# An inverse DFT with its operand, its copies and its last stage laid out anew

## The chip, the cores and the metric

The kernel runs on one core of one Trainium2 chip. The metric is the device time of one execution in microseconds. The core has a matrix engine (TensorE, in the profile PE, with its weight loads as PEld), a vector engine (VectorE, DVE), an activation engine (ScalarE, ACT), GpSimd (POOL) and SyncE (SP), which here only issues DMAs. Each engine works through its own queue in order; engines wait for one another by semaphores.

## The reference, cut to what matters

`u` is 2048 positions by 512 channels. A layer norm gives `xn`; a state-space convolution and a one-token expert run on it, and their product is added to `u`.

```python
x = A_u
xn = _layernorm(x, axis=-1)
# s: long convolution of each channel with a kernel K of 2048 taps
dt = jnp.exp(log_dt)[:, None]
P = jnp.exp((dt * A)[:, :, None] * l[None, None, :])
K = jnp.einsum("dn,dnl,dn->dl", Cc, P, dt * Bc).real
Yf = rfft(pad(xn.T)) * rfft(pad(K))
s = irfft(Yf)[..., :L].T + xn * Dskip
# g: silu of xn, where the one token with the highest router score got an FFN added
g = _silu(_B_ref(xn, w_r, w_gate, w_up, w_down))
return x + s * g
```

## The kernel before

All Fourier transforms are matrix products. The 512 channels are worked on in two halves, h = 0 and 1, of 4 x 64 channels (in the code, q counts the four groups of 128 channels, and h is a half of each group). The stages, in the order of the data:

- **norm, router, ffn** give the normalised rows, the chosen row and the gate operand G, which goes through DRAM (`scr_g`).
- **useq, useq2** transform the input in two steps and leave its spectrum in DRAM (`scr_u`); `load_u(h)` brings a half back into `UU[h]`: for each of 32 residues k2, real and imaginary parts on 128 partitions, and a second copy (t = 1) with the two parts exchanged. For h = 0 both copies come by DMA; for h = 1 one comes by DMA and eight on-chip copies make the other.
- **tab, exp, g, q, qc, mm** (together "kgen") build K for each half on ScalarE, VectorE and TensorE; **kx** turns it into the operand `KX[h]`.
- **spec** (`spec(h, ...)`): for each pair of residues kp (16 of them) ten 128x256 matmuls of the table FD with KX give the spectrum of K in a PSUM bank, an evacuation copies it to `KF`, and VectorE multiplies it with UU (stage uum). For h = 0 the product is written over UU, 1024 elements in one instruction; for h = 1 it goes to `Y1` in four instructions of 256 elements, where the columns of one channel lie 4 elements apart.
- **inv** (`inv_a(h)`): the first step of the inverse. For each of 64 channels m two matmuls (t = 0, 1), whose weights are the 128 columns of that channel and whose moving operand is a 128-column table, write every fourth word of a bank; after eight channels four copies of 64 partitions by 512 elements bring the pair of banks to `C`.
- **fin** (`fin_h(h)`): the last step. For each position l1 sixteen matmuls on four column tiles, of 128 rows and 64 columns; the table FB has zeros in half of its rows, so that two groups q share one operand. Then ScalarE copies the result (`TB`), VectorE multiplies by silu(G) and adds the input row (`XR`), and for h = 1 four DMAs per block store 32 partitions each.

`_Graph` records each operation with its buffers and works out the waits from the overlaps of addresses; buffers are placed by hand at offsets from `RA`, `RX`, `RM`, `RQ0`, `RQ1`, `RT`, `RG`, so that two buffers of different stages often share a place, and a write waits for the last read of what lay there. Helpers issue everything, so that lines of the profile are those of helpers: `mm` is L647, `tt` L598, `act` L593, `evac` L626 on ScalarE or L627 on VectorE, `dma` L664. The order of each engine's queue is a table of operation numbers, `ORDER`, made beforehand by a planner from estimated costs. In it fin0 stands within spec1 and inv1, and `g.schedule` only checks it.

Of the kernel before, what the change touches and what calls it, by code (L numbers as in the profile page):

```python
# [16 lines left out]
KB = 1024  # L17
# [323 lines left out]
def tables():  # L341
# [28 lines left out]
    FZ = np.zeros((2, 2, 32, 64, 2, 32))  # L370
    for q in range(2):
        FZ[:, q, :, :, q] = FB.transpose(2, 0, 1, 3)
    FB = FZ.reshape(128, 64, 2, 32)
# [6 lines left out]
        9 8 10 3-4 19 14 13 20 16 15 216 18 212 17 214 148 144 149-150 146 102 97 100 151 147 101 99 143 142 96 145 95 98 155 157 154 156 152-153 222  # L380
        224 218 220 226 228 230 232 236 238 234 240 250 252 242 254 316 256 258 321 260 708 264 262 326 331 709 336 268 341 270 266 346 710 351 711
        713-714 278 712 851 808 804 806-807 803 805 1006 1005 1004 1014 1016 1015 1025 1028 1026 1003 1052 1017 1027 1038 1051 1041 1040 1039""",
    scalar="""
        2 6 5 7 12 11 21 53-54 22 29 55 26 25 30 24 27 57-59 46 450 440 425 34 31 33 444 38 446 435 48 426 452 454 443 424 37 442 439 430 136 449 88
# [4 lines left out]
        592 579 597 578 575 340 338 500 598-599 570 628 577 590 587 574 588 600 345 343 514 576 520 581 348 518 350 595 586 522 596 582 524 584 572  # L389
        528 530 532 534 672 716 719 722 725 639 728 731 643 641 734 737 645 743 740 749 746 755 686 688 761 752 690 758 692 854 698 696 764-765 771  # L390
        700 769-770 776 775 704 777 781-782 786 811-812 789 792 790 879 810 873 794 891 801 885 809 897 802 915 909 797 927 921 939 933 951 823 945
        830 957 959-960 837 963 969 968 972 975 977 980 984 983 989 988 992 848 993 1000 1011 1022 1035 1048 1053-1054""",
    vector="""
        0-1 211 105 103 106 113 104 111 66 71 28 112 107 109 23 117 56 110 62-63 108 118 68 114 65 116 115 64 61 119 36 67 60 70 69 120 32 72 121 73
        122 74 123 75 84 124 76 125 77 126 78-79 127 131 80 128 81 129 82 130 132 83 133-134 85 137-139 86 135 140-141 87 91 90 92-93 89 94 161 164
        159 167 170 173 362 360 364 179 359 367 283 368 184-185 361 186 369 363 373 457 374 188 379 456 376 459 380 190 458 191-193 460 462 385 195
        461 388 464 463 197 466 198-200 465 375 467-468 202 469-472 386 473 205 474 476 475 210 477-478 274-275 479-482 309 484 488 485 506 486-487
        490 489 505 483 503 491-492 244 247 494 493 507 498 245 508 330 496 509-510 246 335 249 203 511-512 603 606 604 607 605 609 516 608 610-611
        671 613 612 615 614 616-617 619 618 673 621 630 620 622-623 625 624 626-627 526 629 631 633 632 272 635 276 634 277 674 636-637 646-647 649
        648 650-654 656 655 658 657 535 660 659 662 661 664 663 676 666 665 675 668 667 670 669 678 677 679-680 682 681 684 683 729 741 726 732 717  # L400
        747 735 744 762 720 738 723 759 753 750 756 857 694 853 766-767 855 859 772 774 706 858 702 852 707 779 784 780 787 785 867 791 871 861 856
        862-863 796 814 880-881 870 883 865 882 868 864 818 875 869 816 876 795 894 892 874 877 815 903 895 817 905 887 906 886 889 888 799 898 800
        900-901 899 893 912 904 913 910 930 911 907 925 929 924 922 916 941 940 942 918 917 923 934 931 919 928 943 937 953 955 954 952 936 824 935
        946 948 947 949 825 831-832 958 964 962 965 967 970 974 973 979 978 982 985 987 990 994 838 995 839 849-850 1001-1002 1012-1013 1023-1024
        1049-1050 1036-1037""",
    gpsimd="""
        447 390 389 536-537 42 39 41 40 43-44 594 279""",
    tensor="""
        45 47 158 160 163 166 162 169 165 172 168 171 175 178 174 181 49 177 282 51 180 183 286 187 290 280 189 294 284 194 298 196 288 302 201 292
        204 306 296 206-209 310 300 213 215 217 304 219 221 223 308 225 227 229 231 314 312 233 235 319 317 237 324 239 322 241 243 327 497 329 495  # L410
        332 501 334 499 337 339 515 344 251 253 255 519 342 513 349 347 257 259 517 261 263 521 525 523 527 529 531 533 265 267 269 271 715 718 721
        724 638 727 730 642 640 733 736 644 742 739 748 745 754 685 687 760 751 689 757 691 697 695 693 763 768 699 773 705 701 703 778 783 860 866
        788 813 793 878 872 798 890 884 902 896 914 908 926 920 938 932 950 819-822 944 826-829 956 961 833-836 966 840 842 841 843-845 971 976 981
        986 991 846-847 996-999 1007-1010 1018-1019 1031 1020-1021 1032 1029-1030 1033-1034 1044-1045 1042-1043 1046-1047""",
# [7 lines left out]
def build(nc, A_u, A_A_re, A_A_im, A_B_re, A_B_im, A_C_re, A_C_im, A_log_dt, A_Dskip,  # L422
# [52 lines left out]
    with g.ctx:  # L475
# [80 lines left out]
        G0 = g.buf("G0", RQ1 + 16 * KB, [4, 2, 16, 64], BF16)  # L556
        FB = g.buf("FB", RQ1 + 32 * KB, [64, 2, 32], BF16)
# [8 lines left out]
        VM = g.buf("VM", RT, [4, 512], BF16)  # L566
        WR4 = g.buf("WR4", RT + 9 * KB, [128], BF16)
        WRC = g.buf("WRC", RT + 9 * KB + 256, [4], BF16)
        KF = [g.buf(f"KF{i}", RT + 9 * KB + 1024 * i if i < 3 else RQ0 + 37 * KB + 1024 * (i - 3) if i < 8 else RM + 1024 * i, [4, 128], BF16) for i in range(16)]
# [608 lines left out]
        spec(0, range(16), FD, 0)  # L1178

        g.stage = "inv0"  # L1180
        inv_a(0)
        g.stage = "ldz"
        load(FB(FB.a.reshape(-1)), t_fb.ap(), 128 * 8192)
        g.stage = "ldg"
# [109 lines left out]
```

## Time and profile before

| | us |
|---|---|
| median of 3 runs | 220.4 (218.86 to 221.02) |
| profiled execution | 220.46 |
| its span, first to last instruction | 218.6 |
| TensorE busy | 166.0 (76%) |
| VectorE busy | 189.4 (87%) |
| ScalarE busy | 161.3 (74%) |

Times in the views run from the start of the span. A row of a timeline has start, length, engine, line, operation, output and operands, the shape, and how many instructions are merged. `128*20 128x42` at a matmul are the weights' rows and columns and the moving operand's rows and columns. Matmuls overlap, so the slot of one in a stream is what counts: the length of the stream less one duration, by the number less one. The granted clock is the share of TensorE's full clock.

The end of the kernel by the chain of waits is TensorE from 123 us on, then the copies and products of the last step, then the stores.

### The profile page before, as it was taken

The page shows a single profiled execution, that of the slowest core. Times are in us where ns is not written, and L with a number is a line of the kernel's source. Part 1 is how long each engine was busy: PE and PEld are TensorE (multiplying, and loading weights), DVE is VectorE, ACT ScalarE, POOL GpSimd, SP SyncE. Part 2 cuts the span into 40 slices and gives each one's busy share as a digit, 9 for nine tenths or more (in the row PEclk, how much of TensorE's full clock was granted, in tenths as well). Part 3 has the DMA queues.
Part 4 walks back from the last instruction along what each step waited for, and adds up shares of the span by engine and source line. Part 5 has one row for each costly group of instructions (what it writes and reads, how often), then busy time and mean ns, then how long its engine had stood idle before and what let it go on. Part 6 is the DMA issues. An engine that isn't in the chain of part 4 may idle for free.

```text
span 218.6 us, 6958 instructions
## 1 busy us (share of the span) xinstructions
PE 166.0 (76%) x2995; PEld 134.7 (62%) x2995; DVE 189.4 (87%) x408; ACT 161.3 (74%) x318; POOL 13.8 (6%) x17
## 2 busy tenths in 40 slices
PE   0150787799868768879957499989999997999440
PEld 0140676573654346657746488889889886988330
DVE  3999988998999999999999999476779999767970
ACT  2899999999999999999722144464689977556630
POOL 2021430000000000000000620000000000000000
PEclk9995555555965559999988799997999999999755
DMA  6990579700455896969999972059980000000076
GB/s 216 396 374 0 138 142 200 294 3 0 151 178 175 232 352 177 308 179 264 310 286 213 363 294 108 3 126 390 208 240 3 3 0 4 3 0 3 3 199 187
DMA packets 21142, 36.76 MB, mean 168 GB/s; under 512 B 1944, under 2 KB 16888, under 8 KB 20088
## 3 DMA queue, kind: packets, MB, share of 16 engines
q1 hardware_dynamic: 20120, 35.60, 54.2%
q10 hardware_dynamic: 960, 0.72, 1.0%
q8 instruction: 23, 0.38, 0.7%
q14 instruction: 7, 0.06, 0.1%
q0 software_dynamic: 32, 0.00, 0.0%
HBM read 25.83 MB, written 8.39 MB: 157 GB/s over the span
## 4 chain that ended last, share of the span: by engine, by line
PE 41%; DVE 35%; ACT 13%; issue 5%; DMA 2%; SPq 0%; DVEq 0%
PE PB L647 41%; DVE TT L598 8%; DVE QQ L598 8%; DVE Y L598 4%; DVE GG L598 3%; ACT E L593 2%; DMA X<-in_A_u_dram 2%; DVE ST L760 2%; ACT AU L626 2%; ACT TB L593 2%; ACT SL L593 2%; DVE LST L616 1%; ACT XT L626 1%; DVE QQ L1024 1%; ACT QQ L593 1%
## 5 line engine op out<-in xcount | busy, mean ns | idle before, releaser
L647 PE MATMUL PB<-KX,FD 128*128 128x256 bf16 x320 | 38.7, 281 | 0.0
L647 PEld LDWEIGHTS PB<-KX,FD 128*128 128x128 bf16 x320 | 31.6, 101 | 5.8 <-ACT KX L626 0.4
L647 PE MATMUL PB<-QQ,GG 128*20 128x42 bf16 x1024 | 25.0, 263 | 9.7 <-DVE QQ L598 5.2
L647 PEld LDWEIGHTS PB<-QQ,GG 128*20 128x20 bf16 x1024 | 21.4, 124 | 13.5 <-issue 6.8
L627 DVE CAST C<-PB 64x512 bf16<-64x512 f32 x30 | 20.7, 689 | 9.5 <-PE PB L647 8.2
L626 ACT ACTIVATE C<-PB 64x512 bf16<-64x512 f32 x34 | 20.1, 592 | 11.9 <-PE PB L647 10.7
L626 ACT ACTIVATE KF<-PB 128x512 bf16<-128x512 f32 x29 | 17.3, 598 | 13.7 <-PE PB L647 12.9
L598 DVE TENSOR_TENSOR TT<-GG,MB 128x2048 bf16<-128x2048 bf16 (+3 forms) x32 | 24.3, 787 | 0.3
L593 ACT ACTIVATE QQ<-TH 128x256 bf16<-128x256 f32 x64 | 22.5, 427 | 0.0
L593 ACT ACTIVATE E<-AR 128x256 bf16<-128x256 f32 x64 | 22.3, 426 | 0.0
L598 DVE TENSOR_TENSOR QQ<-QQ,E 128x1024 bf16<-128x1024 bf16 (+2 forms) x16 | 19.6, 1252 | 0.0
L647 PE MATMUL PB<-CB,XZN 32*128 32x64 bf16 x256 | 15.8, 327 | 4.4 <-ACT AU L626 3.5
L647 PEld LDWEIGHTS PB<-CB,XZN 32*128 32x128 bf16 x256 | 12.8, 203 | 7.0 <-ACT AU L626 5.0
L647 PE MATMUL PB<-CB,UU 128*128 128x128 bf16 x128 | 17.0, 338 | 0.0
L626 ACT ACTIVATE KE<-PB 128x336 bf16<-128x336 f32 x13 | 6.0, 464 | 13.7 <-PE PB L647 13.7
L647 PE MATMUL PB<-AU,F2U 64*128 64x256 bf16 x128 | 12.6, 342 | 4.4 <-ACT UST L626 3.6
L647 PEld LDWEIGHTS PB<-CB,UU 128*128 128x128 bf16 x128 | 15.7, 185 | 0.4 <-issue 0.2
L598 DVE TENSOR_TENSOR GG<-TT 128x1024 bf16<-128x1024 bf16 (+3 forms) x38 | 15.1, 434 | 0.4
L647 PE MATMUL PB<-CB,Y 128*128 128x128 bf16 x128 | 14.6, 313 | 1.1 <-DVE Y L598 1.1
L626 ACT ACTIVATE AU<-PB 128x1024 bf16<-128x1024 f32 x14 | 14.2, 1041 | 0.5 <-PE PB L647 0.5
L647 PEld LDWEIGHTS PB<-CB,Y 128*128 128x128 bf16 x128 | 13.5, 137 | 1.6 <-DVE Y L598 1.2
L598 DVE TENSOR_TENSOR Y<-UU,KF 128x256 bf16<-128x256 bf16 x64 | 14.0, 283 | 0.4 <-ACT KF L626 0.3
(133 smaller groups left out, 287.5 us busy)
## 6 DMA issues: line engine op xcount, KB each, us to landing
FD<-c_fd SPq DMA_DIRECT2D x4, 1280.0 KB, 7.6
scr_u<-UST SPq DMA_DIRECT2D x8, 512.0 KB, 5.2
UU<-scr_u SPq DMA_DIRECT2D x2, 2048.0 KB, 15.4
XZN<-XN SPq DMA_DIRECT2D x16, 128.0 KB, 4.2
scr_g<-XN SPq DMA_DIRECT2D x4, 512.0 KB, 7.2
UU<-scr_u SPq DMA_DIRECT2D x2, 1024.0 KB, 11.3
XR<-in_A_u_dram SPq DMA_DIRECT2D x4, 512.0 KB, 14.6
G<-scr_g SPq DMA_DIRECT2D x1, 2048.0 KB
```

Source lines behind the costliest of these rows:

```text
L593: g.op(AC, lambda e: e.activation(out=out.ap, in_=in_.ap, func=func, **kw), w=[out], r=r, cost=cost(AC, out, 0.71), table=table, tokr=tokr ...
L598: g.op(eng, lambda e: e.tensor_tensor(out=out.ap, in0=a.ap, in1=b.ap, op=op), w=[out], r=[a, b], cost=cost(eng, out, rate))
L616: g.op(eng, lambda e: e.scalar_tensor_tensor(out=out.ap, in0=a.ap, scalar=x, in1=b.ap, op0=op0, op1=op1), w=[out], r=r, cost=cost(eng, out ...
L626: g.op(AC, lambda e: e.activation(out=out.ap, in_=in_.ap, func=ACT.Copy), w=[out], r=[in_], cost=cost(AC, out, 0.71) + 80, alt=(DV, lambda ...
L627: alt=(DV, lambda e: e.tensor_copy(out=out.ap, in_=in_.ap), cost(DV, out, 1.05) + 95))
L647: ins = e.matmul(o_.ap, lhsT=l_.ap, rhs=r_.ap, start=st, stop=sp, **kw)
L760: g.op(DV, lambda e, b=b: e.bn_stats(ST6(ST6.a[b]).ap, X0(X0.a[b]).ap), w=[ST6(ST6.a[b])], r=[X0(X0.a[b])], cost=620)
L1024: lambda e: e.tensor_scalar(out=out.ap, in0=in_.ap, scalar1=-1.0, scalar2=None, op0=ALU.mult), cost(DV, out, 0.3))
```

## The change

- The product with the spectrum is written, for both halves, to a new buffer `Y[h]` in the order [t, channel, q, k2]: the 128 columns of one channel are adjacent. Each of the 16 steps takes two instructions of 512 elements; the elements of a step lie 128 elements (256 bytes) apart in the output.
- The inverse reads `Y[h][t, m]`; its result is copied as 128 partitions by 1024 elements, with the last copy of h = 1 in two halves.
- The last step runs once, behind both halves: FB without zeros and repeated on four groups of 32 partitions, sixteen 32-row, 32-column tiles, with a moving operand of 2 x 64 columns; six blocks of 2 or 4 positions; one store of 128 partitions per block. The last product reads PSUM directly.
- Buffers have new places: Y0 at RM (where kgen's tables E, TH, MB lay), Y1 over UU0 and GG, C in the second halves of UU0 and UU1's places, UU1 at RQ1 (kgen's Q1) with its load in two parts, G0 in two parts and two loads, FB at RX + 8 KB, XR at RM (Y0's place), KF8 to 15 at RT (kgen's scratch TT).
- `ORDER` is new for all engines.

```diff
-    FZ = np.zeros((2, 2, 32, 64, 2, 32))
-    for q in range(2):
-        FZ[:, q, :, :, q] = FB.transpose(2, 0, 1, 3)
-    FB = FZ.reshape(128, 64, 2, 32)
+    FB = np.tile(FB, (4, 1, 1, 1))
...
-        C = apart("C", RM, RM2, [2, 64, 64])
-        Y1 = g.buf("Y1", RQ0, [2, 16, 4, 32, 4], BF16)
-        UU = [g.buf("UU0", RQ0, [2, 4, 32, 64], BF16), apart("UU1", RM2, RQ1, [4, 32, 64])]
+        C = apart("C", RQ0 + 16 * KB, RQ1, [2, 64, 64])
+        Y = [g.buf("Y0", RM, [2, 64, 4, 32], BF16), apart("Y1", RQ0, RG, [64, 4, 32])]
+        UU = [g.buf("UU0", RQ0, [2, 4, 32, 64], BF16), g.buf("UU1", RQ1, [2, 4, 32, 64], BF16)]
...
-                if h == 0:
-                    uv = uu(uu.a[:, :, 2 * kp:2 * kp + 2].reshape(2, 4, 128))
-                    tt(DV, uv, uv, kf(bc(kf.a[None], (2, 4, 128))), ALU.mult)
-                else:
-                    for kk in range(2):
-                        for t in range(2):
-                            k2 = 2 * kp + kk
-                            tt(DV, Y1(Y1.a[t][:, :, k2].transpose(1, 0, 2)), uu(uu.a[t, :, k2].reshape(4, 16, 4)), kf(kf.a[:, 64 * kk:64 * kk + 64].reshape(4, 16, 4)), ALU.mult)
+                for t in range(2):
+                    tt(DV, Y[h](Y[h].a[t, :, :, 2 * kp:2 * kp + 2].transpose(1, 2, 0)), uu(uu.a[t, :, 2 * kp:2 * kp + 2]), kf(kf.a.reshape(4, 2, 64)), ALU.mult, 1.05)
...
-                        lst.append((pr(pr.a.reshape(2, 128, 4)[i // 4, :, i % 4]), uu(uu.a[t, :, :, m].reshape(128)) if h == 0 else Y1(Y1.a[t, m // 4, :, :, m % 4].reshape(128)), CB(cb(("FA1", "FA2")[t])), t == 0, t == 1, None))
-                mm(lst, 60 if h else 92)
-                for tq in range(2):
-                    for ri in range(2):
-                        evac(C(C.a[h, tq, :, 8 * x8:8 * x8 + 8].reshape(64, 2, 4).transpose(1, 0, 2), 64 * ri, 64), pr(pr.a.reshape(2, 2, 64, 4)[:, ri], 64 * tq, 64))
+                        lst.append((pr(pr.a.reshape(2, 128, 4)[i // 4, :, i % 4]), Y[h](Y[h].a[t, m].reshape(128)), CB(cb(("FA1", "FA2")[t])), t == 0, t == 1, None))
+                mm(lst, 60)
+                for i in range(2) if h == 1 and x8 == 7 else (None,):
+                    cv = C.a[h, :, :, 8 * x8:8 * x8 + 8].reshape(128, 2, 4).transpose(1, 0, 2)
+                    pv = pr.a.reshape(2, 128, 4)
+                    evac(C(cv if i is None else cv[i]), pr(pv if i is None else pv[i]))
...
+        SET = ((0, 1), (2, 3))
+        for kb, (r0, nr) in enumerate(((0, 2), (2, 4), (6, 4), (10, 2), (12, 2), (14, 2))):
+            prs = [PP[k] for k in SET[kb % 2]]
...
+                for ri in range(2):
+                    for a in range(4):
+                        for q in range(4):
+                            k_ = blk(q)
+                            l1 = 16 * a + r0 + b4
+                            lst.append((k_(k_.a[:, b4], 32 * a, 32), FB(FB.a[l1, ri], 32 * q, 32), C(C.a[:, ri, l1], 32 * q, 32), ri == 0 and r0 < 12, None, (32 * q, 32 * a)))
+                mm(lst, 15)
+            for qp in range(2):
...
+                if r0 == 14 and qp:
+                    for q in range(2):
+                        tt(DV, t_(t_.a[n_ * q:n_ * q + n_].reshape(2, 64 * nr)), prs[qp](prs[qp].a[512 * q:512 * q + n_].reshape(2, 64 * nr)), G0(gv[2 * q:2 * q + 2]), ALU.mult)
+                else:
+                    act(t_(t_.a[0:2 * n_].reshape(2, n_)), ps, ACT.Copy)
+                    tv = t_(t_.a[0:2 * n_].reshape(4, 64 * nr))
+                    tt(DV, tv, tv, G0(gv), ALU.mult)
+                xv = XR(XR.a[r0:r0 + nr, 256 * qp:256 * qp + 256].reshape(nr, 4, 64).transpose(1, 0, 2))
+                tt(DV, xv, t_(t_.a[0:256 * nr].reshape(4, nr, 64)), xv, ALU.add)
+            store(_dma_rows(out, 512 * r0, [[8192, 4], [32768, 32], [1, 512 * nr]]), XR(XR.a[r0:r0 + nr].reshape(-1)), 128 * 1024 * nr)
```

In the new order, behind the end of kgen, the queues hold: on TensorE spec1 mixed with inv0, then inv1, then fin; on VectorE the products of uum0, then those of uum1 with five of the UU1 copies; on ScalarE all KF copies, all eight inv0 copies, five of the inv1 copies, and the four silu of G: the first within spec1, the second ahead of the last inv1 copy, the third behind that copy, the fourth behind the first two copies of fin; on SP the two UU1 loads, G0, FB, G0, XR and six stores.

More of the change, by code (lines that the diff above doesn't have):

```diff
@@ L1181, in build @@
         inv_a(0)
+        g.stage = "spec1"
+        load_u(1)
+        spec(1, range(16), FD, 0)
+        g.stage = "inv1"
+        inv_a(1)
+        g.stage = "fin"
         g.stage = "ldz"
@@ L1198, in build @@
             ts(DV, VM(VM.a[r], 0, 4), V4(None, 0, 4), CF(CF.a[m0 + 4 + r:m0 + 5 + r], 0, 4), None, ALU.mult, rate=0.4)
+        g.stage = "fin"
         nt = 0
[L1203 to L1217 removed]
+        SET = ((0, 1), (2, 3))
@@ L1230, in fin_h @@
[L1230 to L1240 removed]
+                ps = prs[qp](prs[qp].a.reshape(2, 512)[:, :n_])
+                gv = G0.a[2 * qp:2 * qp + 2, :, r0:r0 + nr].reshape(4, 64 * nr)
```

124 lines of the change are left out of this document (53 added, 71 removed), and 4 rows, old and new, of the table scalar.

## The prediction

> **What bounds the kernel now.** I read the busy shares first (DVE 87%, PE 76%, neither full), then the chain of waits, which says what is late in each stretch, then busy time by stage, then the timelines of the stretches that the change touches. From the chain (start, us, what):
>
> ```profile
> 123.01 20.99 PE PB L647 x435
> 144.52 28.71 PE PB L647 x264
> 179.51 4.62 DVE Y L598 x22
> 185.80 16.00 PE PB L647 x228
> 204.92 1.02 ACT TB L593
> 212.86 0.42 DVE XR L598
> ```
>
> By stage (us, then PE, PEld, DVE, ACT, POOL busy, granted clock, DMA share, GB/s):
>
> ```profile
> 132.00:144.50 12.50, 11.96 (x313) 10.30 (x310) 8.68 (x16) 5.64 (x12) 0.00 (x0) 1.00 0.06 22
> 144.50:185.80 41.30, 40.18 (x486) 35.99 (x487) 35.20 (x101) 32.16 (x43) 0.00 (x0) 0.96 0.44 129
> 185.80:201.80 16.00, 16.00 (x240) 14.73 (x244) 11.49 (x17) 9.36 (x16) 0.00 (x0) 1.00 0.01 2
> 201.80:213.30 11.50, 5.59 (x296) 4.11 (x296) 9.64 (x16) 6.31 (x8) 0.00 (x0) 0.64 0.37 101
> ```
>
> From 132 to 201.8 us TensorE is full (40.2 of 41.3 us, 16.0 of 16.0); behind that stands a tail of copies, products and stores to 218.6. The change pays where it shortens TensorE's line or the tail. What it may spend is VectorE's slack in 132 to 185.8.
>
> **The inverse matmuls.** Their pace decides most. Timelines, granted clocks, and durations (min/median/max ns):
>
> ```profile
> 192.83 8.95 PE L647 MATMUL PB<-CB,Y 128*128 128x128 bf16 x80
> 146.94 3.73 PE L647 MATMUL PB<-CB,UU 128*128 128x128 bf16 x17
> 33.12 0.61 PE L647 MATMUL PB<-CB,WC 128*128 128x128 bf16 x4
> 194.00:200.00 6.00, 6.00 (x58) 1.00 0.01 3
> 147.20:150.30 3.10, 3.10 (x17) 0.50 0.90 338
> 33.10:33.50 0.40, 0.40 (x6) 0.50 1.19 149
> L647 PE MATMUL PB<-CB,UU x128: 273/314/502, 146.6 to 169.6; 128*128 128x128 bf16 x128
> L647 PE MATMUL PB<-KX,FD x320: 272/273/421, 106.2 to 183.7; 128*128 128x256 bf16 x160
> L647 PEld LDWEIGHTS PB<-CB,UU x128: 166/173/253, 146.6 to 169.5; 128*128 128x128 bf16 x128
> L647 PEld LDWEIGHTS PB<-CB,Y x128: 111/139/139, 185.8 to 201.4; 128*128 128x128 bf16 x128
> ```
>
> A Y matmul takes a slot of (8.95 - 0.31)/79 = 0.109 us (0.31 is its own length, the median 314 ns). At the half clock a UU one takes (3.73 - 0.50)/16 = 0.20 us: the slot goes with the clock. WC, 128 columns packed on both sides, takes (0.61 - 0.31)/3 = 0.10 us at the half clock, so some 0.05 at the full one. What makes the inverse twice as slow? Either the operand's columns (64 elements apart in UU, 4 in Y), which the change puts together, or the output, written to every fourth word of a bank, which it leaves. UU and Y load their weights at different lengths (173 against 139 ns) and yet have one slot; and a UU matmul that queued for nothing lasts 273 ns, as the 256-column FD does (272), with half the columns. Both point to the output. I take 0.109 us, unchanged: 16 in 1.75 us, a half's inverse 14.0 us. The other end, 0.05 to 0.06, is the second case below.
>
> The Trainium skill ("TensorE: Matmul & The Clock Gate", Back-to-back issue gap) gives about 81 ns for a stream of loads and 128-column matmuls; by it, as an estimate, each inverse would take 10.4 us and the sum below would end 7.2 us earlier; the trace has 109.
>
> **VectorE: the product with the spectrum (stage uum).**
>
> ```profile
> 131.21 0.83 DVE L598 TENSOR_TENSOR QQ<-TT 128x576 bf16<-128x576 bf16 x2
> 131.95 4.92 DVE L598 TENSOR_TENSOR UU<-UU,KF 128x1024 bf16<-128x1024 bf16 x8
> 177.16 6.97 DVE L598 TENSOR_TENSOR Y<-UU,KF 128x256 bf16<-128x256 bf16 x33
> L598 DVE TENSOR_TENSOR SL<-SL,SL 128x512 f32<-128x512 f32 x6 | 4.1, 684 | 0.8 <-ACT SL L593 0.8
> L598 DVE TENSOR_TENSOR TB<-TB,G 128x512 bf16<-128x512 bf16 x2 | 0.8, 422 | 0.4 <-ACT TB L593 0.4
> L1131 DVE COPY UU<-UU 64x2048 bf16<-64x2048 bf16 x7 | 4.7, 687 | 0.1
> ```
>
> 16 products of 1024 elements (slot 4.92/8 = 0.61) and 64 of 256 (6.97/33 = 0.21) become 64 of 512 whose output steps 256 bytes per element. No row shows such a write. The lower bound is the packed bf16 row (422 ns), the upper twice the fp32 row of that size (684 ns). I take the fp32 row itself, one element at a time; it is as long as the 1024-element bf16 product, so its slot is 0.61 too. VectorE goes from 9.8 + 13.5 to 64 x 0.61 = 39.0 us: 15.7 us more.
>
> The Trainium skill ("VectorE: DVE Perf Modes", The perf-mode tier table and What auto-detection actually checks) says that a tensor_tensor does two elements a cycle only where every operand steps by one: that speaks against this change. Its 1x figure, 691 ns without overlap, is an estimate here, and agrees with the fp32 row's 684.
>
> What hides it: kgen ends at 132.04 (131.21 + 0.83). The new order puts two products ahead of that (1.2) and shifts some earlier evacuations to VectorE (one XT, one UST, fewer KE, KS and XN: about 1 us): 134.2. Behind stand 62 products and 5 of the 8 UU copies, 37.8 + 5 x 0.62 = 40.9 us: done at 175.1, 177 with waits. TensorE must come later than that.
>
> **TensorE to the second inverse.** From 134.2:
>
> ```profile
> 139.84 1.50 PE L647 MATMUL PB<-QQ,GG 128*20 128x42 bf16 x64
> 137.55 2.36 PE L647 MATMUL PB<-KX,FD 128*128 128x256 bf16 x20
> 144.52 2.12 PE L647 MATMUL PB<-CB,KE 128*64 128x80 bf16 x32 [0.56 <-ACT KE L626]
> 151.91 0.67 PE L647 MATMUL PB<-CB,KE 128*64 128x64 bf16 x8
> 155.89 0.29 PE L647 MATMUL PB<-CB,KS 64*128 64x64 bf16 x4
> ```
>
> Two kgen blocks 3.0; six spectra (10 FD matmuls each: (2.36 - 0.27)/19 = 0.110 apiece, 1.09) 6.5; the kx stage 4.8 (2.1 for its first 32 and 2.7 for six smaller groups, of which the first and the last stand here); 16 spectra of the second half 17.5; the first inverse 14.0; the four-row matmul 0.4: 46.2 us. The kx chain of matmul, copy, matmul is now covered by spectra only, since the first inverse must wait for all of uum0, so I add 1.5 of gaps: the second inverse starts at 181.9 (185.8 before; fin0's matmuls are gone from ahead of it). VectorE is 5 us earlier, so its 15.7 us cost nothing; without that cover they cost what exceeds 5.
>
> **Inverse copies.**
>
> ```profile
> L627 DVE CAST C<-PB 64x512 bf16<-64x512 f32 x30 | 20.7, 689 | 9.5 <-PE PB L647 8.2
> L626 ACT ACTIVATE C<-PB 64x512 bf16<-64x512 f32 x34 | 20.1, 592 | 11.9 <-PE PB L647 10.7
> L626 ACT ACTIVATE UST<-PB 128x1024 bf16<-128x1024 f32 x14 | 14.1, 1036 | 0.0
> ```
>
> 64 copies of 64 rows, 40.8 us, become 15 of 128x1024 (1.04 on ACT) and two halves, 17 us. All but the last run beside matmuls (one copy per 1.75 us), so only the last counts, 0.7 us. The second inverse ends at 195.9, its C at 196.6.
>
> **The tail.** fin0 used to run inside TensorE's line; now both halves run behind the last copy. Its matmuls:
>
> ```profile
> 183.97 0.73 PE L647 MATMUL PB<-C,FB 128*32 128x64 bf16 x64
> L593 ACT ACTIVATE TB<-PB 128x1024 bf16<-128x1024 f32 x7 | 7.1, 1021 | 3.7 <-PE PB L647 3.5
> L593 ACT ACTIVATE TB<-PB 128x512 bf16<-128x512 f32 x2 | 1.2, 597 | 0.7 <-PE PB L647 0.7
> L593 ACT ACTIVATE G<-G 128x2048 bf16<-128x2048 bf16 x4 | 7.6, 1925 | 0.0
> 207.42 9.32 SPq L664 DMA_DIRECT2D out_dram<-XR  x18
> ```
>
> Four column tiles take 64 columns each at once today, (0.73 - 0.20)/63 = 8 ns a matmul. There are again 512, with 128 columns but on 16 tiles: between 4 ns (16 together) and 17 ns (4 together), 2 to 9 us in all; at 32 to 64 to a copy pair even the slow end stays beside ScalarE. ScalarE then bounds: one silu of G stands ahead of the first copy (1.9, to 198.5), then 2 copies of 512 (1.2), a silu (1.9), 4 of 1024 (4.1), 5 of 512 (3.0): 10.2, to 208.7. VectorE's 24 products, 8 x 0.61 + 16 x 0.35 (422 ns less the 0.07 by which neighbours overlap) = 10.5 from the first copy on, keep step; the last ones add 1.0: 209.7. The stores go from 18 on SP (9.32/18 = 0.52 each, and they end the kernel: last issue over at 216.7) to six: issue 0.5 and landing with the closing wait 2.3: 212.5. Against 218.6 that is 6.1 us less.
>
> **Waits by the new places.** KF8 to 15 lie in kgen's scratch: their ScalarE copies wait to 134.2, with KE copies queued behind, 1 us. UU1 lies in Q1, so its two loads wait for the last kgen block, about 138.3 (the queue held nothing else then). XR takes Y0's place, so its load waits for the first inverse, about 180, the stores behind it on SP; first needed at 198. G0 and FB follow UU1 early.
>
> The profiled execution took 220.46 us, 1.86 outside its span, the median of three is 220.4: 212.5 + 1.86 = 214.4.
>
> **Rivals.** (B) The packed columns free the inverse: 0.056 us a slot. TensorE is ready at 175, VectorE at 177 sets the start, and the second inverse then goes at the pace of its copies: 0.9 for the first 16 matmuls, 5.1 for five copies in a row on ScalarE, 1.2 for one on VectorE, 0.9 for the last 16, 0.7 for the halves and 0.8 of hand-overs, 9.6 in all. C is there at 186.6, 10 us earlier: 204.4. For it: WC. Against it: UU and Y with one slot. (C) The strided write costs more. From 181.9 - 134.2 - 3.1 - 2 = 42.6 us over 62 products, VectorE sets the start from 0.69 us a product on, the gain is gone at 0.79, at 0.9 the time is 228, at 1.2 246. Against it: the C copies write runs of 8 bytes and last 689 ns, as an fp32 row does. (D) The UU1 loads come late.
>
> ```profile
> UU<-scr_u SPq DMA_DIRECT2D x2, 1024.0 KB, 11.3
> ```
>
> VectorE reaches the first UU1 copy at 148. At 338 GB/s (row above) both land by 147; with 11.3 us and one behind the other, at 153, and the products in line behind the copies hold up the first inverse by 5: 219.4.
>
> **The numbers.** Forecast 0.55 (210 to 218: gaps on TensorE 0 to 5 us, tail within 2), B 0.22 (203 to 208), D 0.10, C 0.13. The range leaves out C and the edge of D: 203.5 to 220. A measurement here tells 1% (2.2 us) from no change. Faster by more: B and nearly all of the forecast, 0.75; same: D and the forecast's edge, 0.12; slower: C, 0.13.
>
> **What would show it.** CB,Y at 16 in 1.75 us (B: under 1.0); Y products near 690 ns, 0.61 apart, ended before the second inverse starts at about 182; C copies 128x1024; ScalarE without a gap from 197 to 208, six stores. I am wrong if Y products last over 0.85 us, if VectorE or a UU1 load stands ahead of the inverse in the chain, or if FB matmuls hold up the tail's copies.

## The result, and the profile after

The changed kernel takes 337.4 us (median of 4 runs, 336.56 to 339.84) against 220.4 for the kernel before: 1.534 times as long, 95% interval 1.523 to 1.546. Its profiled execution took 336.56 us, its span is 334.7. The prediction had 214.4. Medians and ranges here leave out single runs over 1.5% slower than the fastest of their kernel. In the changed kernel the helpers stand four lines higher: `tt` is L594, `mm` L643, `act` L589, `evac` L622 and L623, `dma` L660.

The chain of waits after (start, us, what):

```profile
138.53 50.93 DVE Y L594 x22
...
201.74 36.58 DVE Y L594 x16
...
241.13 20.88 DVE Y L594 x9
262.74 6.32 PE PB L643 x43
269.06 38.08 DMA XR<-in_A_u_dram
310.65 1.20 DVE TB L594 x2
```

Before, TensorE carried this stretch; now VectorE's products do. At the end the chain leaves them: the first inverse, whose last matmuls end at 269.06, must have read Y0 before XR can be loaded to its place, and the last products wait for that load. By stage (us, then PE, PEld, DVE, ACT, POOL busy, granted clock, DMA share, GB/s): products, second inverse, last step, and what follows the last product.

```profile
138.00:282.00 144.00, 55.50 (x498) 46.23 (x486) 143.75 (x67) 33.54 (x45) 0.00 (x0) 0.71 0.13 42
282.00:299.30 17.30, 15.98 (x128) 15.70 (x128) 5.70 (x10) 7.60 (x8) 0.00 (x0) 0.87 0.26 63
299.30:317.50 18.20, 8.07 (x520) 5.42 (x520) 10.97 (x26) 11.24 (x13) 0.00 (x0) 0.61 0.21 56
317.50:334.70 17.20, 0.00 (x0) 0.00 (x0) 0.00 (x0) 0.00 (x0) 0.00 (x0) 0.50 0.23 87
```

VectorE is busy for 143.75 of 144 us; then, at the end, no engine computes for 17 us while DMA runs at a share of 0.23. The groups behind it (busy us, mean ns of one, idle before):

```profile
L594 DVE TENSOR_TENSOR Y<-UU,KF 128x512 bf16<-128x512 bf16 x64 | 147.5, 2655 | 0.1
...
L622 ACT ACTIVATE KF<-PB 128x512 bf16<-128x512 f32 x32 | 18.5, 598 | 103.6 <-DVE Y L594 86.6
```

A product lasts 2655 ns; its slot is (50.93 - 2.66)/21 = 2.30 us, 4.5 ns an element. The copies to KF wait 86.6 us for products to free their buffers, and TensorE waits behind them. The timeline of the end:

```profile
282.60 15.98 PE L643 MATMUL PB<-CB,Y 128*128 128x128 bf16 x128 [13.27 <-DVE Y L594]
...
298.62 0.69 DVE L623 CAST C<-PB 128x512 bf16<-128x512 f32 x1 [0.52 <-PE PB L643]
...
299.36 1.73 PE L643 MATMUL PB<-C,FB 32*32 32x128 bf16 x171 [0.78 <-DVE C L623]
...
303.41 1.49 PE L643 MATMUL PB<-C,FB 32*32 32x128 bf16 x128 [2.32 <-issue]
...
307.14 0.76 PE L643 MATMUL PB<-C,FB 32*32 32x128 bf16 x53 [2.24 <-issue]
...
307.23 0.76 DVE L594 TENSOR_TENSOR XR<-TB,XR 128x512 bf16<-128x512 bf16 x2 [4.79 <-DMA XR<-in_A_u_dram]
...
308.02 15.09 SPq L660 DMA_DIRECT2D out_dram<-XR  x6
...
316.66 0.76 DVE L594 TENSOR_TENSOR XR<-TB,XR 128x512 bf16<-128x512 bf16 x2
```

Against the prediction's sum, whose span was 212.5:

| | predicted | after | difference |
|---|---|---|---|
| second inverse starts | 181.9 | 282.6 | +100.7 |
| from there to the last C copy's end | 14.7 | 16.7 | +2.0 |
| from there to the last product's end | 13.1 | 18.1 | +5.0 |
| from there to the end of the span | 2.8 | 17.3 | +14.5 |

These make up the 122.2 us by which the span was missed. The 2.0 of the second row are the start of the second inverse, behind TensorE's wait of 13.27 us: in its first 4.0 us, at a granted clock of 0.53, TensorE works on 21 matmuls (0.19 us each), in its last 8.6, at 1.00, on 79 (0.109). The experiments take the other three one by one.

### The profile page after: what moved, and what is told of

Read it like the earlier page. It is cut to its first block, busy times and chain, and to the rows that moved or that the text cites. A ratio compares the mean times of both kernels' runs of the same rounds, so it can differ in the third digit from the quotient of the medians.

```text
span 334.7 us, 6871 instructions
## 1 busy us (share of the span) xinstructions
PE 176.9 (53%) x2991; PEld 141.2 (42%) x2991; DVE 290.0 (87%) x366; ACT 161.0 (48%) x307; POOL 10.6 (3%) x17
## 4 chain that ended last, share of the span: by engine, by line
DVE 58%; DMA 15%; ACT 11%; PE 7%; issue 3%; SPq 1%; DVEq 0%; ACTq 0%
DVE Y L594 37%; DMA XR<-in_A_u_dram 11%; PE PB L643 7%; DVE TT L594 6%; DVE QQ L594 5%; ACT E L589 4%; DVE GG L594 2%; DMA XZN<-XN 2%; DVE XR L594 2%; DMA X<-in_A_u_dram 1%; DVE TB L594 1%; ACT AU L622 1%; ACT UST L622 1%; DVE UU L1131 1%; SPq L660 1%
## 5 line engine op out<-in xcount | busy, mean ns | idle before, releaser
L594 DVE TENSOR_TENSOR Y<-UU,KF 128x512 bf16<-128x512 bf16 x64 | 147.5, 2655 | 0.1
L643 PE MATMUL PB<-KX,FD 128*128 128x256 bf16 x320 | 46.8, 310 | 51.9 <-ACT KF L622 50.0
L622 ACT ACTIVATE KF<-PB 128x512 bf16<-128x512 f32 x32 | 18.5, 598 | 103.6 <-DVE Y L594 86.6
L643 PEld LDWEIGHTS PB<-KX,FD 128*128 128x128 bf16 x320 | 34.0, 111 | 61.9 <-ACT KF L622 51.7
L643 PE MATMUL PB<-CB,Y 128*128 128x128 bf16 x256 | 34.8, 353 | 39.1 <-DVE Y L594 39.1
L643 PEld LDWEIGHTS PB<-CB,Y 128*128 128x128 bf16 x256 | 33.5, 157 | 40.1 <-DVE Y L594 39.7
L643 PE MATMUL PB<-QQ,GG 128*20 128x42 bf16 x1024 | 24.4, 263 | 6.5 <-issue 4.3
L622 ACT ACTIVATE C<-PB 128x1024 bf16<-128x1024 f32 (+1 forms) x14 | 13.9, 994 | 24.7 <-PE PB L643 24.7
L643 PEld LDWEIGHTS PB<-QQ,GG 128*20 128x20 bf16 x1024 | 21.3, 123 | 10.3 <-issue 7.4
L594 DVE TENSOR_TENSOR TT<-GG,MB 128x2048 bf16<-128x2048 bf16 (+3 forms) x32 | 24.0, 784 | 0.1
L589 ACT ACTIVATE QQ<-TH 128x256 bf16<-128x256 f32 x64 | 23.1, 429 | 0.0
L589 ACT ACTIVATE E<-AR 128x256 bf16<-128x256 f32 x64 | 21.5, 411 | 0.0
L594 DVE TENSOR_TENSOR QQ<-QQ,E 128x1024 bf16<-128x1024 bf16 (+2 forms) x16 | 19.6, 1254 | 1.1 <-ACT E L589 1.1
L643 PE MATMUL PB<-CB,XZN 32*128 32x64 bf16 x256 | 15.7, 324 | 4.1 <-ACT AU L622 2.6
L643 PE MATMUL PB<-AU,F2U 64*128 64x256 bf16 x128 | 13.3, 360 | 8.2 <-ACT UST L622 4.8
L643 PEld LDWEIGHTS PB<-CB,XZN 32*128 32x128 bf16 x256 | 13.0, 202 | 6.7 <-ACT AU L622 4.0
L622 ACT ACTIVATE AU<-PB 128x1024 bf16<-128x1024 f32 x15 | 15.0, 1022 | 1.0 <-PE PB L643 0.9
L594 DVE TENSOR_TENSOR GG<-TT 128x1024 bf16<-128x1024 bf16 (+3 forms) x38 | 15.2, 431 | 0.2
L622 ACT ACTIVATE UST<-PB 128x1024 bf16<-128x1024 f32 x13 | 13.4, 1031 | 0.1
L643 PE MATMUL PB<-CB,XN 128*64 128x128 bf16 x128 | 8.3, 314 | 9.3 <-DVE LST L612 7.3
L623 DVE CAST C<-PB 128x1024 bf16<-128x1024 f32 (+1 forms) x3 | 3.1, 1047 | 11.5 <-PE PB L643 11.5
L622 ACT ACTIVATE KE<-PB 128x336 bf16<-128x336 f32 x14 | 6.2, 450 | 12.5 <-PE PB L643 12.4
```

The source lines that it names most:

```text
L589: g.op(AC, lambda e: e.activation(out=out.ap, in_=in_.ap, func=func, **kw), w=[out], r=r, cost=cost(AC, out, 0.71), table=table, tokr=tokr ...
L594: g.op(eng, lambda e: e.tensor_tensor(out=out.ap, in0=a.ap, in1=b.ap, op=op), w=[out], r=[a, b], cost=cost(eng, out, rate))
L622: g.op(AC, lambda e: e.activation(out=out.ap, in_=in_.ap, func=ACT.Copy), w=[out], r=[in_], cost=cost(AC, out, 0.71) + 80, alt=(DV, lambda ...
L623: alt=(DV, lambda e: e.tensor_copy(out=out.ap, in_=in_.ap), cost(DV, out, 1.05) + 95))
L643: ins = e.matmul(o_.ap, lhsT=l_.ap, rhs=r_.ap, start=st, stop=sp, **kw)
```

## The experiments

### Single operations by themselves

Each product goes from the same packed inputs to places a given step apart, two to four times; matmuls and transfers follow. The heart of it, S being the step in elements:

```diff
+        for S in (16, 32, 64, 96, 128, 130, 132, 136, 144, 256):
+            rep(f'step{S}el', [(8, 1), (64, S)], 2 if S == 16 else 4, 8)
+        for r in (2, 4, 8):
+            rep(f'runs{r}el', [(8 // r, r), (64, 128), (r, 1)], 4, 8, idims=[(8 // r, 64 * r), (64, r), (r, 1)])
```

> Single operations by themselves; all of the reference's computation is left out. VectorE products of 512 bf16 elements whose output elements lie a given step apart; the changed kernel's own product (step 128) took 2656 ns. Theory 1 (each write that lands alone in a short stretch of memory costs, 4.5 ns, at any distance): packed 420 ns; steps of 2 and 4 elements near 690; steps of 8 to 256, and 130 to 144 too, 2400 to 2650; runs of 2 elements 1200 to 1350; runs of 4 and 8 under 700; fp32 output at step 128 as slow as bf16; a one-input copy as slow on VectorE. Theory 2 (a step of 256 bytes meets one bank each time): 128 and 256 near 2650, but 96, 130, 132, 136, 144 near 690. Theory 3 (a 2-byte write costs because it is less than a word): fp32 output at step 128 near 690, all bf16 steps from 2 on slow. Theory 4 (the reading, not the writing): strided outputs near 690, strided input with a packed output slow. Matmuls of 128 weights by 128 columns at the full clock: if the output at every fourth word sets the slot, packed output 0.055 us at any step of the weights, every fourth word 0.109; if the weights' step sets it, 0.109 at steps 4 and 64, 0.055 at 1. Copies of a pair of banks: 1.02 us on ScalarE both ways of reading. Transfers of 2 MB: with the pattern whose outer dimension is 4, 38 us if the pattern is the cause, 6 to 12 us with 128 rows and as four of 32 rows; all near 10 us if other traffic was the cause.

Groups of instructions (busy us, mean ns of one); the tile's name has the step or the run in elements, `runs2across` reads its inputs across, `step128fp` writes fp32, `CO<-BG,IN` reads one input at a step of 128 and writes packed:

```profile
L331 DVE TENSOR_TENSOR step96el<-IN 128x512 bf16<-128x512 bf16 x4 | 10.7, 2970 | 0.0
L331 DVE TENSOR_TENSOR step128el<-IN 128x512 bf16<-128x512 bf16 x4 | 10.5, 2890 | 0.0
...
L331 DVE TENSOR_TENSOR step8el<-IN 128x512 bf16<-128x512 bf16 x4 | 9.4, 2658 | 0.0
...
L331 DVE TENSOR_TENSOR step130el<-IN 128x512 bf16<-128x512 bf16 x4 | 8.9, 2501 | 0.0
...
L331 DVE TENSOR_TENSOR step4el<-IN 128x512 bf16<-128x512 bf16 x4 | 4.7, 1324 | 0.0
L331 DVE TENSOR_TENSOR CO<-BG,IN 128x512 bf16<-128x512 bf16 x4 | 3.8, 1005 | 0.0
L331 DVE TENSOR_TENSOR step128fp<-IN 128x512 f32<-128x512 bf16 x4 | 3.6, 1021 | 0.0
L331 DVE TENSOR_TENSOR runs2across<-IN 128x512 bf16<-128x512 bf16 x4 | 2.5, 693 | 0.0
L331 DVE TENSOR_TENSOR runs2el<-IN 128x512 bf16<-128x512 bf16 x4 | 2.1, 644 | 0.0
L331 DVE TENSOR_TENSOR packed<-IN 128x512 bf16<-128x512 bf16 x4 | 1.4, 420 | 3.9 <-DMA IN<-in_A_u_dram 3.9
...
L331 DVE TENSOR_TENSOR runs4el<-IN 128x512 bf16<-128x512 bf16 x4 | 1.4, 419 | 0.0
L331 DVE TENSOR_TENSOR step2el<-IN 128x512 bf16<-128x512 bf16 x2 | 1.3, 720 | 0.0
```

Steps of 8 elements (16 bytes) and more are all slow, 2446 (a step of 144) to 2970 ns, 130 as well as 128: theory 2 falls. Reading at a step of 128 costs 1005 ns: theory 4 falls. Theories 1 and 3 each have half. The cost grows with the step only up to 16 bytes (720, 1324, 2658 ns for 4, 8 and 16 bytes), as theory 1 has it. But two elements written one behind the other to neighbouring places bring it to 644 ns (theory 1 had 1200 to 1350), and a 4-byte element at the same step costs 1021, so it is the lone 2-byte write that is dear, as theory 3 has it. (The 1005 and the 1021 were taken while ScalarE made strided copies of its own, from 134.05 to 143.36 us, so alone they may be lower.) By slots: (9.4 - 2.66)/3 = 2.25 us for 512 lone writes 16 bytes apart, 4.4 ns each; (4.7 - 1.32)/3 = 1.13 us at 8 bytes, again 4.4 ns per 16 bytes; runs of 2 read across (2.5 - 0.69)/3 = 0.60 us; runs of 4 cost no more than packed. Over all steps from 16 to 512 bytes the slot is 2.09 to 2.56 us, 4.1 to 5.0 ns a write. One thing went against theory 1: a one-input copy to places 128 elements apart lasts 1.75 to 2.58 us on VectorE, but four of them start between 141.2 and 144.7, 1.2 us apart, half the slot of a product. Why is not shown.

The Trainium skill ("SBUF — State Buffer", the box on cachelines under Door 1) says that accesses which cross to a new 16-byte line with fewer than two hits on it pay a penalty, and gives no price. The flat cost from 16 bytes on agrees; that a step of 8 bytes (two hits to a line) still costs 1324 ns, and that 4-byte writes each on a line of its own cost well under half of the 2-byte ones, does not follow from it.

Matmuls, 48 begun in each window (the count in brackets has those under way at its edges too): output packed with the weights' columns adjacent, 4 apart, and 64 apart, then output at every fourth word with columns adjacent and 4 apart.

```profile
15.94:18.62 2.68, 2.68 (x52) 1.00 0.02 6
18.62:21.30 2.68, 2.68 (x52) 1.00 0.00 0
21.30:25.69 4.39, 4.39 (x51) 1.00 0.02 4
...
41.37:46.61 5.24, 5.24 (x50) 1.00 0.00 0
46.61:51.85 5.24, 5.24 (x50) 1.00 0.00 0
```

At the full granted clock a slot is 2.68/48 = 0.056 us with a packed output and 5.24/48 = 0.109 at every fourth word, whether the columns are adjacent or 4 apart; 64 apart costs 0.091 with a packed output. At every second word it is 5.20/48 = 0.108. The output sets the slot, as the prediction read it. Reading the bank across costs the copies nothing: on ScalarE three copies in order lasted 1001 to 1347 ns and three across 1027 to 1046, on VectorE 1214 to 1225 and 1211 to 1214.

A 2 MB load by the pattern with an outer dimension of 4 was issued at 156.0 us, and the next load, which waits for it, at 194.8: 38.7 us with nothing else at work. The same bytes as 128 rows took 7.7 us, as four pieces of 32 rows 12.3. In the middle of the first and of the third (DMA share and GB/s are the last two columns):

```profile
156.00:190.00 34.00, 0.00 (x0) 0.00 (x0) 0.01 (x1) 0.00 (x0) 0.00 (x0) 0.50 0.24 56
...
204.00:212.00 8.00, 0.00 (x0) 0.00 (x0) 0.00 (x0) 0.00 (x0) 0.00 (x0) 0.50 1.01 219
```

A share of 0.24 is about 4 of 16 engines. The Trainium skill ("DMA: Bandwidth & Descriptors", How many engines) says that the number of engines is the largest one up to 16 that divides both patterns' slowest dimension: 4 here, and the trace agrees.

### The two repairs, apart and together

Transfers in pieces (`e1_pieces`), and runs of 4 in the product as the kernel before had them (`e2_runs`); `e3_runs_pieces` has both. The numbers in `ORDER` follow. In the kernels with runs of 4 the helpers stand two lines lower than in the changed kernel (`mm` is L645).

```diff
-        load(XR(XR.a.reshape(-1)), _dma_rows(A_u, 0, [[8192, 4], [32768, 32], [1, 8192]]), 128 * 16384)
+        for a in range(4):
+            load(XR(XR.a.reshape(-1), 32 * a, 32), _dma_rows(A_u, 8192 * a, [[32768, 32], [1, 8192]]), 32 * 16384)
...
-            store(_dma_rows(out, 512 * r0, [[8192, 4], [32768, 32], [1, 512 * nr]]), XR(XR.a[r0:r0 + nr].reshape(-1)), 128 * 1024 * nr)
+            for a in range(4):
+                store(_dma_rows(out, 8192 * a + 512 * r0, [[32768, 32], [1, 512 * nr]]), XR(XR.a[r0:r0 + nr].reshape(-1), 32 * a, 32), 32 * 1024 * nr)
```

```diff
-        Y = [g.buf("Y0", RM, [2, 64, 4, 32], BF16), apart("Y1", RQ0, RG, [64, 4, 32])]
+        Y = [g.buf("Y0", RM, [2, 16, 4, 32, 4], BF16), apart("Y1", RQ0, RG, [16, 4, 32, 4])]
...
-                    tt(DV, Y[h](Y[h].a[t, :, :, 2 * kp:2 * kp + 2].transpose(1, 2, 0)), uu(uu.a[t, :, 2 * kp:2 * kp + 2]), kf(kf.a.reshape(4, 2, 64)), ALU.mult, 1.05)
+                    for kk in range(2):
+                        k2 = 2 * kp + kk
+                        tt(DV, Y[h](Y[h].a[t][:, :, k2].transpose(1, 0, 2)), uu(uu.a[t, :, k2].reshape(4, 16, 4)), kf(kf.a[:, 64 * kk:64 * kk + 64].reshape(4, 16, 4)), ALU.mult)
```

> The changed kernel with the load of XR and each of the six stores again as four transfers of 32 rows, as the kernel before has them; products as changed. Theory (the pattern with an outer dimension of 4 makes these transfers slow): XR is there before the last step needs it (the wait of 4.8 us goes) and the stretch from the last product to the end falls from 17.3 to 3 to 5 us: 19 us less in all, 337.4 - 19 = 318 us. Rival (their size or what else moves then makes them slow): less than 3 us of change, 335 to 338. Products stay at 2.3 us a slot in both.

324.9 us (323.74 to 325.68): 12.5 us less, not 19. Its last rows:

```profile
300.60 0.69 DVE L623 CAST C<-PB 128x512 bf16<-128x512 f32 x1 [0.52 <-PE PB L643]
...
316.89 0.75 DVE L594 TENSOR_TENSOR XR<-TB,XR 128x512 bf16<-128x512 bf16 x2
```

The span is 323.6. From the last product to the end there are 6.0 us in place of 17.3, which is the cause at work. But from the last C copy to the last product it is 16.4 us, only 1.8 less, though the wait for XR of 4.8 is gone: something else stood behind that wait (the half of the last step, below, follows it up).

> The changed kernel with the product written as the kernel before wrote it for its second half, for both halves: runs of 4 elements, four instructions of 256 elements a step, a channel's columns 4 elements apart; all else as changed, the slow transfers too. Theory (the lone 2-byte writes cost all that was lost up to the second inverse): products at 0.21 us a slot, 128 of them 27 us; the second inverse starts at 180 to 185; then XR, loaded from about 180 on in 38 us, is there at 218 and bounds the rest, which took 26.7 us behind it in the changed kernel: span 240 to 247, time 242 to 250. Rival (the new order and places cost too, VectorE late by more than the products): second inverse later than 195. Rival on the inverse: if the adjacent columns helped TensorE at all, its slot goes from 0.109 up.

251.3 us (248.83 to 252.04), a little over the 242 to 250 expected. The second inverse and the load of XR:

```profile
181.62 14.16 PE L645 MATMUL PB<-CB,Y 128*128 128x128 bf16 x128
```

```profile
181.41 38.07 DMA XR<-in_A_u_dram
```

As expected, the products are no longer the bound, and the slow load sets the rest, landing at 219.5 of a span of 247.0. The inverse's slot is (14.16 - 0.31)/127 = 0.109 us with columns 4 apart.

> Both edits together: runs of 4 in the product, transfers of 32 rows. If the products and the transfers are all that the prediction had wrong, its sum comes out but for the known rests: 212.5, and 2 for 24 stores in place of six and 2 for the half clock in the second inverse: span 214 to 218, time 216 to 221, the same as the kernel before within 1%. If other parts of the change cost, over 224; if the four-group last step and the wide copies gain more than I counted, under 213.

221.8 us, 1.009 times the kernel before (1.004 to 1.015), just over the 216 to 221 expected. The second inverse again, the last copy and the last product:

```profile
181.64 14.16 PE L645 MATMUL PB<-CB,Y 128*128 128x128 bf16 x128
```

```profile
195.84 0.69 DVE L625 CAST C<-PB 128x512 bf16<-128x512 f32 x1 [0.52 <-PE PB L645]
...
213.07 0.75 DVE L596 TENSOR_TENSOR XR<-TB,XR 128x512 bf16<-128x512 bf16 x2
```

With the two prices put right the prediction's sum holds up to the tail: second inverse at 181.6 (181.9 predicted), its C at 196.5 (196.6). The tail is then 17.3 us (13.1 predicted) and the end 5.6 (2.8), which uses up the gain of 6 us. In that tail the chain of waits holds two stops of TensorE:

```profile
198.31 2.22 issue
200.54 1.34 PE PB L645 x128
201.88 2.94 issue
```

Together they are 5.2 us, more than the 4.2 by which the tail is too long.

### The same places, another order of writing; and the bank packed

```diff
-                    tt(DV, Y[h](Y[h].a[t, :, :, 2 * kp:2 * kp + 2].transpose(1, 2, 0)), uu(uu.a[t, :, 2 * kp:2 * kp + 2]), kf(kf.a.reshape(4, 2, 64)), ALU.mult, 1.05)
+                    tt(DV, Y[h](Y[h].a[t, :, :, 2 * kp:2 * kp + 2].transpose(1, 0, 2)), uu(uu.a[t, :, 2 * kp:2 * kp + 2].transpose(0, 2, 1)), kf(kf.a.reshape(4, 2, 64).transpose(0, 2, 1)), ALU.mult, 1.05)
```

> The changed kernel with transfers of 32 rows, its own operand with a channel's columns adjacent, and one word turned in the product: the same 64 instructions of 512 elements go through the places in the order group, channel, residue in place of group, residue, channel, so that the two neighbouring 2-byte elements are written one behind the other and both inputs are read across (64 elements apart). By the single operations (runs of 2 read across, 693 ns, slot 0.60 us, against 2656 and 2.3) the products take 64 x 0.60 = 39 us in place of 147: the prediction's own 0.61, and its sum should hold: VectorE done with the products at 177 to 180, second inverse starting at 180 to 184, span 217 to 222, time 219 to 224, level with the run whose products write runs of 4. Rival (in this place, with weights, copies and transfers at work beside it, or with two free inputs, the order of writing doesn't matter): products over 1.5 us, time over 280.

223.1 us, 1.012 times the kernel before (1.007 to 1.018). Its products (min/median/max ns):

```profile
L594 DVE TENSOR_TENSOR Y<-UU,KF x64: 676/686/801, 130.6 to 181.1; 128x512 bf16<-128x512 bf16 x64
```

The same 512 places get the same values from the same instruction count, with the columns adjacent as the change wants them; only the order within an instruction is turned (and with it the order of reading, which alone does not make runs of 2 faster: 693 ns across, 644 in order), and 2655 ns become 686. Against `e1_pieces` this line is the whole edit: 324.9 us become 223.1. That settles what the products' cost is. The inverse starts at 183.5 and its slot stays 0.109: adjacent columns don't help it.

```diff
-                        lst.append((pr(pr.a.reshape(2, 128, 4)[i // 4, :, i % 4]), Y[h](Y[h].a[t, m].reshape(128)), CB(cb(("FA1", "FA2")[t])), t == 0, t == 1, None))
+                        lst.append((pr(pr.a.reshape(2, 4, 128)[i // 4, i % 4]), Y[h](Y[h].a[t, m].reshape(128)), CB(cb(("FA1", "FA2")[t])), t == 0, t == 1, None))
...
-                    pv = pr.a.reshape(2, 128, 4)
+                    pv = pr.a.reshape(2, 4, 128).transpose(0, 2, 1)
```

This edit is in three kernels: on the last one (`e5_pairs_bank`), on the one with runs of 4 (`e6_runs_bank`), and, with the same turn in its copies, on the kernel before (`e7_before_bank`).

> The last kernel with the inverse's output packed in its bank (128 adjacent words per channel in place of every fourth word) and the copy reading the bank across. By the single operations: matmul slot 0.056 us in place of 0.109, copies unchanged at 0.9 to 1.0 us. Each inverse falls from 14 to about 7.2 us on TensorE. VectorE's products (39 us behind 134) then set the start of the second inverse, near 177 to 180, and its copies its pace (8 of 0.9 to 1.0, on two engines): C done at 186 to 189, the tail of 23 us of the runs with pieces behind it: span 209 to 212, time 211 to 214. Rival (the adjacent columns, not the bank, were to make the inverse fast, and the output's step costs nothing in this stream): slot stays 0.109, no change.

> Runs of 4 in the product, transfers of 32 rows, and the inverse's output packed in its bank; the columns of a channel are 4 elements apart, not adjacent. Slot 0.056 us as with adjacent columns (single operations: 56 ns at weight steps of 1 and 4). Products 27 us instead of 39, so TensorE, not VectorE, sets the start of the second inverse: 7 us earlier than the 180 of the run without it, and it takes 8 instead of 16: span 219.4 - 7 - 7 = 205 to 208, time 207 to 211. If adjacent columns matter in this stream after all, its slot is above that of the run with pairs.

> The kernel before with one edit: the inverse's output packed in its bank, its four copies reading the bank across. Slot of the first half's matmuls (weights 64 elements apart) 0.091 in place of 0.109, of the second half's (4 apart) 0.056. The second half's inverse then goes at the pace of its four copies of 64 rows per eight channels, 1.2 to 1.3 us on two engines, in place of 1.75: 16.0 us becomes 10 to 12; the first half saves 2: 6 to 8 us in all, time 212 to 215. Rival (copies or products bound it in any case): within 2 us of 220.

Times and ratios to the kernel before: 212.65 us, 0.965 (0.961 to 0.968), with pairs; 213.4, 0.970 (0.965 to 0.975), with runs of 4; 213.5, 0.968 (0.965 to 0.971), for the kernel before with this edit alone. Inverse matmuls (ns) and a stretch of the second inverse, with pairs:

```profile
L643 PE MATMUL PB<-CB,Y x256: 219/219/230, 157.4 to 185.1; 128*128 128x128 bf16 x128
```

```profile
176.54 1.96 PE L643 MATMUL PB<-CB,Y 128*128 128x128 bf16 x32 [0.21 <-DVE Y L594]
...
178.73 1.98 PE L643 MATMUL PB<-CB,Y 128*128 128x128 bf16 x32 [0.22 <-ACT C L622]
```

A matmul now takes (1.96 - 0.22)/31 = 0.056 us, and TensorE waits for copies in place of the copies for TensorE. With pairs and on the kernel before the times are as expected. With runs of 4 I had expected 207 to 211, but the second inverse started no earlier than with pairs (176.4 against 176.5), so VectorE's 12 us fewer bought nothing: TensorE itself was busy for 41.0 of the 42.4 us from 134 on (40.9 of 42.5 with pairs). The kernel before gets all of this gain from two edited lines; of the change itself nothing measurable is left beside them.

### Half of the last step, and copies by turns

```diff
-                for ri in range(2):
+                for ri in range(1):
```

> The kernel with pairs, pieces and the packed bank, with half of the last step's matmuls left out (the second of the two sums, 256 of 512; the output is not the reference's). There the stretch from the last C copy (185.9) to the last product (about 203) takes 17.4 us where the prediction's sum has 13.1; TensorE stops three times for 1 to 2.4 us with no releaser shown, after some 128 matmuls each, and the trace has five loads of code of 16.5 KB (256 instructions, 128 matmuls with their weight loads) in it. Theory (TensorE runs through its code faster than the code comes): half the code, so one stop of 1 to 2.4 us in place of three, and the stretch is 3 to 5 us shorter: last product near 199, time 208 to 210. Rival (ScalarE's copies and silus bound the stretch, as the prediction had it): last product within 1 us of before, time 212 to 214.

206.9 us in one run (span 205.0), under the 208 to 210 expected. TensorE and the last copy and product:

```profile
182.07 3.09 DVE L623 CAST C<-PB 128x1024 bf16<-128x1024 f32 x3 [4.25 <-PE PB L643]
...
187.64 1.36 PE L643 MATMUL PB<-C,FB 32*32 32x128 bf16 x117 [1.88 <-issue]
...
191.50 0.34 PE L643 MATMUL PB<-C,FB 32*32 32x128 bf16 x16 [2.50 <-ACT TB L589]
...
199.32 0.75 DVE L594 TENSOR_TENSOR XR<-TB,XR 128x512 bf16<-128x512 bf16 x2
```

There are two stops in place of three (0.99, 2.39 and 2.06 us in the whole kernel), and 14.9 us from the last copy to the last product (185.2 to 200.1) in place of 17.5 (186.0 to 203.5): 2.6 us, a little under the 3 expected, and less than in any kernel with the whole last step (16.4 to 19.4). So the number of the last step's matmuls holds up the copies, which the prediction had excluded. In the whole kernel the chain holds all three stops, here none: it runs on ScalarE to 190.5, then on VectorE's products and additions to the end. VectorE waited 1.62 us there for a copy behind a silu, close to the 1.8 by which 14.9 still exceeds the 13.1.

That TensorE stops because its code comes too slowly has its timing for it. The trace's DMA packets have loads of code of 16 KB. In the kernel with pairs and a packed bank three of them end at 186.33, 190.12 and 193.49 us, and the three stops end 1.30, 1.23 and 1.32 us later, at 187.63, 191.35 and 194.81. The nine kernels with the new last step have 21 stops of 0.99 to 2.94 us among its matmuls, the one above at 191.50 too, and each ends 1.2 to 1.5 us after such a load. No run changed the loads and nothing else, so this cause is likely, not shown.

The last kernel takes the one with pairs and a packed bank, whole, and changes `ORDER` and the last two stores' queue: scalar `792 794 894 870 874 878 882 885`, vector `872 876 880 884`, and

```diff
-                store(_dma_rows(out, 8192 * a + 512 * r0, [[32768, 32], [1, 512 * nr]]), XR(XR.a[r0:r0 + nr].reshape(-1), 32 * a, 32), 32 * 1024 * nr)
+                store(_dma_rows(out, 8192 * a + 512 * r0, [[32768, 32], [1, 512 * nr]]), XR(XR.a[r0:r0 + nr].reshape(-1), 32 * a, 32), 32 * 1024 * nr, eng=SP if r0 < 14 or a < 2 else AC)
```

> The kernel with pairs, pieces and the packed bank, its second inverse's copies taken in turns by ScalarE and VectorE (there five ran on ScalarE one behind the other, and TensorE waited for them), the second silu moved ahead of them, and the last two stores issued by ScalarE. Theory: its second inverse of 9.4 us goes at TensorE's pace, 16 matmuls in 1.0 us, 7.5 to 8.0 in all with hand-overs; the stores end 1 us earlier: span 209.0 - 1.6 - 1 = 206.4, time 209 to 211, 0.95 to 0.96 of the kernel before. Rival (the code of the last step is what TensorE then waits for, so the earlier start is lost in its stops): within 1 us of 212.9.

213.2 us, 0.970 (0.965 to 0.976): no gain. The edit of the order put a silu of 1.9 us ahead of the first copy:

```profile
178.53 1.96 PE L643 MATMUL PB<-CB,Y 128*128 128x128 bf16 x32 [0.21 <-DVE Y L594]
...
178.99 1.91 ACT L589 ACTIVATE G<-G 128x2048 bf16<-128x2048 bf16 x1
...
181.87 1.96 PE L643 MATMUL PB<-CB,Y 128*128 128x128 bf16 x32 [1.37 <-ACT C L622]
```

TensorE then waited 1.4 us for that copy; I had taken ScalarE to be idle at that point. Nor did the turns win time behind it: the matmuls after these 32 begin at 184.05, 2.2 us on, the same distance as with the copies in a row on ScalarE (176.54 and 178.73 above). The stores did end earlier, 4.6 us behind the last product in place of 5.5, but TensorE's three stops in the last step came to 6.7 us in place of 5.4. So the rival's time came true, by more than its own cause. (The profiled executions of the two kernels lie 3.7 us apart, the medians 0.5.)

## Why the prediction was wrong, point by point

- **"The lower bound is the packed bf16 row (422 ns), the upper twice the fp32 row of that size (684 ns). I take the fp32 row itself": this step failed**, and with it the forecast. A product took 2655 ns in a slot of 2.30 us, far above the upper bound. 62 of them at 2.30 for 0.61 are 104.8 us more; about 5 of these were slack, and the second inverse came 100.7 late. "No row shows such a write", the prediction says itself, so twice the nearest row was no bound. Written in pairs, a product does last the 684 ns that it took (686). What I took as evidence against a dear write, C copies that "write runs of 8 bytes", is just the case that costs nothing (runs of 4: 419 ns).
- **Rival C**, the strided write costs more, is what came true, at 2.30 us where I had worked it out up to 1.2. Its rule, that VectorE sets the start of the inverse from 0.69 us a product on, has the right form: 134.2 + 3.1 + 2 + 62 x 2.30 is 281.9, and the inverse started at 282.6.
- **XR's load, which "waits for the first inverse, about 180" and is "first needed at 198", and the stores, "issue 0.5 and landing with the closing wait 2.3": failed.** I priced the stores by their number and the load not at all, and let the new pattern pass, which the diff shows. The load took 38 us; the end took 17.3. In pieces the end still takes 4.6 to 6.0, so with 24 stores that price (2.8) was too small as well.
- **"At 32 to 64 to a copy pair even the slow end stays beside ScalarE": failed by 3 to 6 us.** In the kernels with the whole new last step that have XR in time, 16.4 to 19.4 us pass between the last C copy and the last product, not 13.1, and TensorE stops between its matmuls: 5.2 us of the chain with both repairs, where the tail is 4.2 too long. Halving the matmuls gave 2.6 us back. What was left there is VectorE, which the sum had keep step.
- **The inverse: right.** Its slot stayed 0.109 us at the full granted clock, since the output sets it and columns adjacent or 4 apart don't. Rival B was wrong for the reason given, and the packed bank, which the change leaves out, is what gives 0.056.
- **TensorE's sum of 46.2 us and the 1.5 of gaps: right**, as the run with both repairs shows (181.6 and 196.5 against 181.9 and 196.6; TensorE busy for 46.85 of the 47.4 us from 134.2 on). So were the wide copies (1.02 us on ScalarE, 1.04 in the sum). Rival D did not show: the products were so late that no UU1 load could stand ahead of them, and with both repairs VectorE's products waited only for copies.
- Of the prediction's signs of being wrong, three showed: products over 0.85 us, VectorE ahead of the inverse in the chain, and FB matmuls that hold up the tail's copies.

## What to carry to other kernels

An operand's layout is paid for where it is written: look at what the innermost loop of the writing instruction does in bytes, and let it write at least 4 bytes, better 8, in a row, which may take no more than another order of the same loops. Bound the cost of an access pattern that no row shows by a measurement of that one operation, not by twice the nearest row. When a transfer's pattern changes, read its outermost dimension before its bytes; and when a matmul stream runs at twice its expected slot, look at where its output goes before its operands are moved.

## What the hardware showed that I had not expected

In a product of VectorE a lone 2-byte write to SBUF costs 4.1 to 5.0 ns at every step tried from 16 to 512 bytes and half of that at 8, where a 4-byte write costs (3.6 - 1.02)/3/512 = 1.7 ns and runs of 8 bytes no more than a packed output; in a one-input copy it costs about 2.3 ns (1.2 us for 512). ScalarE pays too: its copies of 512 elements at a step of 128 lasted 2699 ns each. A matmul whose output steps over words of a bank takes two times the packed slot, 0.109 against 0.056 us (0.108 at a step of 2 words), and the copy that reads the bank across is as fast as the one that reads it in order. Among small matmuls TensorE stopped for 1 to 3 us at a time, each time until 1.2 to 1.5 us after a 16 KB load of code.
